# Attention and feed-forward in one kernel: batch one's V in two wide loads spread by TensorE, half-height mask matmuls, column sums in 32-column strips

## The chip, the core and the metric

The kernel runs on one core of one Trainium2 chip. The core has five engines with queues of their own: TensorE (PE: matmuls, and weight loads as PEld), VectorE (DVE), ScalarE (ACT), GpSimd (POOL) and SyncE (SP), which here issues all loads, stores and DMA transposes of the usual path. Sixteen DMA engines move the data. Each engine works through its own list in order; semaphores hold an instruction back until what it reads is there. The metric is device time in microseconds (us), lower is better. The kernel before takes 307.41 us (median of 3 runs, 306.68 to 308.96).

## What is computed

Sliding-window attention over 8 batches, 8 heads, 576 tokens, head size 64, and behind it a feed-forward layer over all 4608 tokens:

```
scores = q @ k.T / 8                      # per batch and head, 576 x 576
scores = where(|i - j| <= 32, scores, -1e9)
attn   = softmax(scores);  x = attn @ v   # heads side by side: 4608 x 512
h      = relu(x @ w_in)                   # w_in  512 x 2048
out    = (s * h * h + b) @ w_out          # w_out 2048 x 512;  s, b are single numbers
```

Since b is one number, its part of the output is b times the column sums of w_out, the same for every token.

## The kernel before, in words

**Planner.** The program is a list of tasks, each for one engine (`add`), with the tiles it reads and writes, an estimated cost and a key. `plan()` sets the tasks in order by list scheduling: it takes again and again the task that can start first by its estimates, and among equals the one with the lower key. `emit()` writes every engine's tasks in that order with the waits that are needed. So a change of one task's cost, key or tiles can move tasks everywhere behind it.

**Batch one (index 0 in the code).** Its q and k are loaded head pair by head pair (`load_pair`, four tokens to a partition, pieces of 1 KB), cast to bfloat16, transposed by TensorE through PSUM (`turn_pair`) and copied to QT and KT. `pair_scores` opens both halves of a PSUM bank with a matmul of the identity by SHUT (L920), which holds 0 inside the window and a huge negative number outside, and adds the scores of 64 x 64 blocks (L914) on top; ScalarE takes the exponential (L959). The last 64 tokens come by a tile of their own ("t", L656) and `late_scores`. V of a batch is handled in units of 128 tokens: `load_v` (L589) loads a unit with one token to a partition, pieces of 64 floats, 256 bytes; `cast_v` (L597, L598) casts it into VB, whose 65th column per head is 1, so that attention-times-V (L839, `av_part`) also gives the softmax's sums. EV0 names the engines of the casts. A unit's result is divided by its sums on VectorE (L861, L863), transposed back by TensorE (L870) and copied to XT (L878), the input of the feed-forward layer. `first_units` puts these steps in order for batch one.

**Order of the loads.** ORDER0 lists what follows q and k of batch one on SyncE: V units v0 to v4, the tail tile t and halves of the first two quarters of w_in (w0a, w0b, w1a, w1b). ORDER1 goes on with batch two (index 1), the other quarters of w_in, and w_out (o0a to o3b). Weights are loaded as float32 into a ring of staging tiles and cast by GpSimd (L564).

**Warm-up matmuls.** `stir` places matmuls without use (L614) at places named in STIR.

**Feed-forward.** `s1` computes 128 rows of x @ w_in per step (L1097), ScalarE the relu (L1104), VectorE the square (L1110). `second` computes the product with w_out for 512 tokens by seven half-size products (L1154) instead of eight; its weights need differences of blocks of w_out (`weight_sums`, L1126). `constant` computes the column sums: 16 matmuls of a matrix of ones by the 16 row blocks of w_out (L1228), two to a task, all added up in one PSUM bank; VectorE multiplies by b into CVEC (L1231), which the output step adds (L1170). FIRST orders the first layer of the first 512 tokens by quarters of w_in.

**Later batches.** From the fourth batch on (PAIRS, LONG) q and k are transposed by DMA (L749), the loads are held back until certain attention steps are done (`paced`), and the last results reach XT by DMA transposes too (L887). The five last batches are treated as one long sequence.

Of the kernel before, what the change touches and what calls it, by code (L numbers as in the profile page):

```python
# [5 lines left out]
F32 = mybir.dt.float32  # L6
# [6 lines left out]
D = 64  # L13
H = 8
# [13 lines left out]
ORDER0 = ("v0", "w0a", "v1", "t", "w0b", "v2", "v3", "w1a", "v4", "w1b")  # L28
# [20 lines left out]
EV0 = ("dve", "act", "pool", "dve", "pool")  # L49
# [6 lines left out]
        ("turn", 3, "q"): 1, ("turn", 3, "k"): 1, ("scores", 2): 1, ("scores", 3): 1, ("av", 0): 1}  # L56
# [266 lines left out]
def bass_sliding_window_symmetric__then__act_starrelu_kernel(  # L323
# [23 lines left out]
    with ExitStack() as es:  # L347
# [49 lines left out]
        IDENT = sb((128, 128), BF16, "ident")  # L397
        GT = [sb((128, 16, 512), BF16, "gt") for _ in range(2)]
# [4 lines left out]
        CVEC = sb((128, DM), F32, "cvec")  # L403
        SB128 = sb((128, 2), F32, "sb128")
# [95 lines left out]

        for i in range(4):
            add("dve", lambda e, i=i: e.tensor_scalar(SHUT[:, i, :], MASK[:, :], -OUTSIDE, OUTSIDE, ALU.mult, ALU.add), 150,
                reads=[("MASK", 0, 0), ("MASK", 0, 64)], writes=[("SHUT", i)], key=-95.0)
# [75 lines left out]
        def load_v(c, u, key, eng, waits=()):  # L579

            vs = number(c, u) % NUNIT
            ts = tiles(c, u)
            at = [tile_at(c, t) for t in ts]
            if len(at) == 2 and at[0][0] == at[1][0]:
                at = [at[0] + (0, 128)]
            else:
                at = [x + (64 * i, 64) for i, x in enumerate(at)]
            n = sum(x[3] for x in at)
            add(eng, [lambda e, b=b, j=j, p0=p0, m=m: e.dma_start(  # L589
                VST[p0:p0 + m, vs, :, :], v[b, :, 64 * j:64 * j + m, :].rearrange("h p d -> p h d"))  # L590
                for b, j, p0, m in at],
                (650.0 if eng == "sp" else 500.0) * len(at), writes=[("VST", vs)], key=key, dma=("l", n // 2, 21.5), waits=waits)
            land["v", c, u] = g.tasks[-1]
# [7 lines left out]

        def load_pair(name, pr, load_key):
# [7 lines left out]
        def stir(spot, res, view, key):  # L610

            n = STIR.get(spot, 0)
            if n:
                add("pe", [lambda e: e.matmul(view, lhsT=ONESW[:, :], rhs=ONESW[:, :].rearrange("p (one c) -> p one c", one=1)  # L614
                                              .to_broadcast((128, 4, 128)), start=True, stop=True) for _ in range(n)],
                    n * (427.0 if spot == ("turn", 0, "q") else 240.0), reads=["ONESW"], writes=[res], key=key - 0.05)
# [19 lines left out]
        def part(b, which, load_key, key, banks, slack):  # L636
# [17 lines left out]
            if which == "t":  # L654
# [3 lines left out]
                    for src, p0 in ((q, 0), (k, 64))], 1000.0, writes=stgr, key=load_key, dma=("l", 64, 21.5))  # L658
# [246 lines left out]
        def pair_scores(b, pr):  # L905
# [3 lines left out]
            if b == 0:  # L909
# [10 lines left out]
            add("pe", [lambda e, hp=hp: e.matmul(bank[:, hp, :], lhsT=IDENT[:, :], rhs=SHUT.rearrange("p u c -> p (u c)"),  # L920
                                                 start=True, stop=False, skip_group_check=True) for hp in (0, 1)],
                440.0, reads=["IDENT"] + [("SHUT", i) for i in range(4)], writes=[(name, 0), (name, 1)], key=key - 0.01)
# [72 lines left out]
        def attention():  # L995
# [228 lines left out]
        def constant():  # L1224

            for i in range(8):
                f0 = 2 * i
                add("pe", [lambda e, fc=fc: e.matmul(SC[:, 0, :], lhsT=ONESW[:, :], rhs=WOUT_BF[:, fc, :],  # L1228
                                                     start=(fc == 0), stop=(fc == 15)) for fc in (f0, f0 + 1)],
                    440, reads=["ONESW", ("Wout", i // 2, i % 2)], writes=[("SC", 0)], accum=i > 0, key=P2[0, 0] - 4.0 + 0.1 * i)  # L1230
            add("dve", lambda e: e.tensor_scalar(CVEC[:, :], SC[:, 0, :], SB128[:, 1:2], None, ALU.mult),  # L1231
                680, reads=[("SC", 0), ("SB128", 1)], writes=[("CVEC", x) for x in (0, 1)], key=P2[0, 0] - 2.0)

# [273 lines left out]
```

## Time and profile before

| | |
|---|---|
| median of 3 runs | 307.41 us |
| profiled execution: time / span in the profile | 308.89 us / 307.2 us |
| TensorE busy (PE) | 294.9 us, 96% |
| weight loads (PEld) | 213.4 us, 69% |
| VectorE / ScalarE / GpSimd busy | 233.2 / 156.7 / 66.4 us |
| moved by DMA | 54.30 MB |
| column sums L1228 | 16 matmuls, 49.5 to 57.6 us |
| mask matmuls L920 | 16 matmuls, 8 pairs |

The span runs from the first to the last instruction of one execution. A line of the timeline gives start, duration, engine, source line, operation, output and input tiles, the shape, and in brackets the idle time ahead of it with what ended it. A matmul's duration contains its way through the array, so that successive matmuls overlap: what one costs in a stream is the distance of the starts. `sc`, `o`, `avn`, `w` are PSUM tiles of two banks each. In the table of stages the numbers are the stretch in us, its length, the busy time of each engine (and its instructions), the granted TensorE clock as a share of full speed, the mean busy share of the DMA engines (over 1 where packets overlap), and GB/s.

### The profile page before, as it was taken

What the parts mean: (1) busy time and instruction counts of PE and PEld (TensorE: products, weight loads), DVE (VectorE), ACT (ScalarE), POOL (GpSimd) and SP (SyncE); (2) the same over time, 40 slices, a digit from 0 to 9 for tenths busy, and PEclk for the clock granted to TensorE, in tenths of its full rate; (3) what the DMA queues carried; (4) which work ended last, traced back from release to release, by engine and by line L of the source; (5) the groups of instructions that cost most, each with busy time, mean ns of one, the idle gap of its engine ahead of it and who ended that gap; (6) DMA issues with size and microseconds to landing.
All of it is one profiled execution on the core that took longest, in us unless ns stands there. A gap on an engine that the chain in (4) does not pass through costs nothing.

```text
span 307.2 us, 8786 instructions
## 1 busy us (share of the span) xinstructions
PE 294.9 (96%) x3837; PEld 213.4 (69%) x3837; DVE 233.2 (76%) x401; ACT 156.7 (51%) x244; POOL 66.4 (22%) x79
## 2 busy tenths in 40 slices
PE   8879899999999999999999999989999999999994
PEld 3458687798888887666766666656666666666783
DVE  3556788699879697989798768995877776566673
ACT  3746775685895564655554544542554433333200
POOL 5344587300000270055047000450000000000000
PEclk9979999999999999999999999999999999999999
DMA  7999999999994997999699679999513110210223
GB/s 204 290 246 302 325 291 370 268 227 273 159 232 125 239 202 160 279 201 178 184 255 198 132 172 273 186 201 150 153 21 88 53 47 31 74 34 2 69 70 107
DMA packets 120152, 54.30 MB, mean 177 GB/s; under 512 B 94816, under 2 KB 115936, under 8 KB 120112
## 3 DMA queue, kind: packets, MB, share of 16 engines
q1 hardware_dynamic: 120112, 53.72, 75.0%
q8 instruction: 31, 0.51, 0.8%
q14 instruction: 9, 0.07, 0.1%
HBM read 36.70 MB, written 9.44 MB: 150 GB/s over the span
## 4 chain that ended last, share of the span: by engine, by line
PE 79%; SPq 4%; DMA 3%; DVE 2%; issue 1%; POOL 0%
PE w L1097 36%; PE o L1154 31%; PE avn L839 4%; SPq L714 3%; DMA stg<-in_moe_w_in_dram 2%; PE sc L1154 2%; PE sc L781 2%; PE avn L870 1%; PE sc L1228 1%; DMA vst<-in_v_dram 1%; DVE outs L1170 1%; DVE gt L1110 1%; SPq L887 0%; SPq L707 0%; POOL win L564 0%
## 5 line engine op out<-in xcount | busy, mean ns | idle before, releaser
L1097 PE MATMUL w<-xt,win 128*128 128x512 bf16 (+4 forms) x832 | 145.7, 316 | 1.3 <-POOL win L564 1.3
L1104 ACT ACTIVATE r<-w 128x512 bf16<-128x512 f32 (+2 forms) x148 | 86.6, 586 | 105.6 <-PE w L1097 103.9
L1097 PEld LDWEIGHTS w<-xt,win 128*128 128x128 bf16 x832 | 75.6, 99 | 35.9 <-POOL win L564 1.9
L1110 DVE TENSOR_TENSOR gt<-r 128x1024 bf16<-128x1024 bf16 (+3 forms) x100 | 63.6, 639 | 24.9 <-ACT r L1104 24.2
L1154 PE MATMUL o<-wout,gt 128*128 128x256 bf16 x528 | 66.5, 273 | 0.0
L1154 PEld LDWEIGHTS o<-wout,gt 128*128 128x128 bf16 x528 | 50.8, 98 | 13.3
L733 POOL CAST nat<-stg 128x1024 bf16<-128x1024 f32 (+2 forms) x28 | 33.7, 1202 | 78.8 <-DMA stg<-in_q_dram 65.0
L809 ACT ACTIVATE ex<-sc 128x1024 bf16<-128x1024 f32 (+1 forms) x29 | 29.7, 1023 | 12.4 <-PE avn L839 10.8
L1154 PE MATMUL o<-tw,gt 128*128 128x256 bf16 x272 | 34.6, 273 | 0.0
L1154 PEld LDWEIGHTS o<-tw,gt 128*128 128x128 bf16 x272 | 26.2, 98 | 7.0
L1170 DVE SCALAR_TENSOR_TENSOR outs<-o,sb,cvec 128x512 f32<-128x512 f32 (+1 forms) x36 | 25.7, 715 | 4.3 <-PE o L1154 4.3
L1170 DVE SCALAR_TENSOR_TENSOR outs<-o,sb,outs 128x512 f32<-128x512 f32 (+1 forms) x27 | 19.3, 716 | 6.7 <-PE o L1154 6.6
L1146 DVE TENSOR_TENSOR gt<-gt 128x1024 bf16<-128x1024 bf16 (+1 forms) x26 | 23.8, 916 | 0.4
L813 DVE TENSOR_TENSOR ex<-ex,mask 128x1024 bf16<-128x1024 bf16 (+1 forms) x29 | 22.5, 775 | 0.6
L863 DVE TENSOR_TENSOR xn<-avn,rec 128x512 bf16<-128x512 f32 (+1 forms) x31 | 21.3, 687 | 0.7
L839 PE MATMUL avn<-vb,ex 64*64 64x65 bf16 x944 | 19.9, 197 | 1.9 <-issue 1.6
L839 PEld LDWEIGHTS avn<-vb,ex 64*64 64x64 bf16 x944 | 13.0, 106 | 11.5 <-issue 8.0
L598 DVE CAST vb<-vst 128x512 bf16<-128x512 f32 (+1 forms) x30 | 13.1, 444 | 9.5 <-DMA vst<-in_v_dram 9.5
L1154 PE MATMUL o<-tw,gsum 128*128 128x256 bf16 x136 | 17.7, 273 | 0.0
L1154 PEld LDWEIGHTS o<-tw,gsum 128*128 128x128 bf16 x136 | 12.8, 98 | 3.3
L1146 DVE TENSOR_TENSOR gsum<-gt 128x1024 bf16<-128x1024 bf16 x18 | 13.2, 731 | 0.3
L878 ACT COPY xt<-avn 128x512 bf16<-128x512 bf16 (+2 forms) x19 | 10.0, 533 | 4.8 <-PE avn L870 4.8
(119 smaller groups left out, 225.4 us busy)
## 6 DMA issues: line engine op xcount, KB each, us to landing
vst<-in_v_dram SPq DMA_DIRECT2D x32, 256.0 KB, 4.8
out_dram<-outs SPq DMA_DIRECT2D x32, 256.0 KB, 3.6
stg<-in_k_dram SPq DMA_DIRECT2D x24, 256.0 KB, 6.5
stg<-in_q_dram SPq DMA_DIRECT2D x5, 1024.0 KB, 6.0
stg<-in_moe_w_in_dram SPq DMA_DIRECT2D x8, 512.0 KB, 7.4
stg<-in_moe_w_out_dram SPq DMA_DIRECT2D x8, 512.0 KB, 7.4
stg<-in_q_dram SPq DMA_DIRECT2D x4, 512.0 KB, 8.2
stg<-in_k_dram SPq DMA_DIRECT2D x4, 512.0 KB, 8.4
```

The costliest lines, as they stand in the source:

```text
L598: (lambda e: e.tensor_copy(VB[0:n, vb, :, 0:D], VST[0:n, vs, :, :])),
L733: (lambda e, dst=dst, src=src: e.tensor_copy(dst, src)),
L809: add("act", lambda e, dst=flat_dst, src=flat_src: e.activation(dst, src, AF.Exp, bias=0.0, scale=0.125), 190 + 0.833 * 512 * len(hs), rea ...
L813: add("dve", lambda e, flat=flat, mask=mask: e.tensor_tensor(flat, flat, mask, ALU.mult), 130 + 0.53 * 512 * len(hs), reads=[("E", ei, hp, ...
L839: return [lambda e: e.matmul(av[64 * x:64 * x + 64, h, 0:D + 1], lhsT=buf[64 * g:64 * g + 64, h % 2, h // 2, c:c + 64], rhs=VB[64 * g:64 * ...
L863: add("dve", lambda e: e.tensor_tensor(XN[xi][0:p1, :].rearrange("p (a c) -> p a c", a=H), av[0:p1, :, 0:D], REC[ri][0:p1, :].rearrange("p ...
L1097: add("pe", [lambda e, g=g, kc=kc: e.matmul(wt[:, g, :], lhsT=WIN_BF[:, kc, (f0 + g) * 128:(f0 + g + 1) * 128], rhs=XT[:, kc, t0 % XR:t0 % ...
L1104: add("act", lambda e: e.activation(rt, wt, AF.Relu, bias=0.0, scale=1.0), 190 + 0.833 * ng * nt, reads=[("W", wb)], writes=[("R1", rb, ha ...
L1110: add("dve", lambda e: e.tensor_tensor(GT[gs][:, f1:f1 + nf, g0:g0 + nt], rr, rr, ALU.mult), 130 + 0.55 * nf * nt, reads=[("R1", rb, x) fo ...
L1146: add("dve", lambda e: e.tensor_tensor(dst, x, y, op), 1240.0 if half is None else 690.0, reads=reads, writes=writes, key=k)
L1154: add("pe", [lambda e, g=g, j=j, dst=dst: e.matmul(dst, lhsT=lhs[:, g, 128 * j:128 * j + 128], rhs=rhs[:, g, :], start=first and g == 0 an ...
L1170: add("dve", lambda e, src=src, dst=dst, other=other: e.scalar_tensor_tensor(dst, src, SB128[:, 0:1], other, ALU.mult, ALU.add), 200 + 1.0 ...
```

## The change

**V of batch one.** Units 0 to 3 (512 tokens) come by two loads "va" and "vb" of 256 tokens, each on all 128 partitions with two neighbouring tokens to a partition, so that a piece is 512 bytes. VectorE casts such a load into a NAT tile (VCAST). Four matmuls with a 0/1 matrix SPREAD, 64 rows each, bring the tokens to one per partition in two PSUM banks (AVN 0 and 1, for both loads), and ScalarE (units 0 and 2) or VectorE (units 1 and 3) copies each unit from PSUM to VB. Unit 4 (64 tokens) is loaded and cast as before. "va" and "vb" stand at the head of ORDER0. The warm-up ahead of the first attention-times-V grows from 1 to 5 matmuls and waits for the first spread.

**Masks.** The opening matmul of `pair_scores` takes 64 rows instead of 128 for each half: TWICE holds two 64 x 64 identities side by side, and the two halves of SHUT are equal, so either half of the rows gives the whole mask.

**Column sums.** Four groups of four matmuls: a group's matmuls write 32-column strips of the array, each its own 32 partitions of one PSUM bank, with ones of 32 columns. ScalarE copies the strips to CVEC, one float32 matmul with a matrix of 1/32 (PART) adds the four strips for all partitions, and VectorE multiplies by b as before.

Two cost entries of the planner are changed as well (27.0 for loads on 64 partitions).

```diff
-ORDER0 = ("v0", "w0a", "v1", "t", "w0b", "v2", "v3", "w1a", "v4", "w1b")
+ORDER0 = ("va", "vb", "w0a", "t", "w0b", "w1a", "v4", "w1b")
-EV0 = ("dve", "act", "pool", "dve", "pool")
+VCAST = ("dve", "dve")
+EV0 = ("act", "dve", "act", "dve", "pool")
-        ... ("scores", 3): 1, ("av", 0): 1}
+        ... ("scores", 3): 1, ("av", 0): 5}
+        for p0 in (0, 64):
+            add("dve", lambda e, p0=p0: e.tensor_copy(
+                TWICE[p0:p0 + 64, :].rearrange("p (a c) -> p a c", a=2),
+                IDENT[p0:p0 + 64, p0:p0 + 64].rearrange("p (a c) -> p a c", a=1).to_broadcast((64, 2, 64))), 120,
+                reads=["IDENT"], writes=[("TWICE", p0)], key=-95.5)
+        def load_runs(y, key):
+            add("sp", lambda e: e.dma_start(
+                VST[:, 2 * y:2 * y + 2, :, :].rearrange("p u h d -> p (u h d)").rearrange("p (h c) -> p h c", h=H),
+                v[0, :, 256 * y:256 * y + 256, :].rearrange("h (p i) d -> p h (i d)", i=2)),
+                600.0, writes=[("VST", 2 * y), ("VST", 2 * y + 1)], key=key, dma=("l", 64, 27.0))
+        def spread_runs(y, key, homes):
+            ni = take("nat", NNAT)
+            rows, eng = NAT[ni], VCAST[y]
...
+            add("pe", [lambda e, i=i, u=u: e.matmul(
+                homes[u][1], lhsT=SPREAD[64 * u:64 * u + 64, 128 * i:128 * i + 128],
+                rhs=rows[64 * u:64 * u + 64, 512 * i:512 * i + 512], start=(i == 0), stop=(i == 1))
+                for i in (0, 1) for u in (0, 1)], 480.0, reads=[("NAT", ni), ("SPREAD", 0), ("SPREAD", 1)],
+                writes=[x[0] for x in homes], key=key)
+            land["spread", y] = g.tasks[-1]
+            for u in (0, 1):
+                vb, eng = number(0, 2 * y + u) % NVB, EV0[2 * y + u]
+                dst, src = VB[:, vb, :, 0:D], homes[u][1].rearrange("p (h d) -> p h d", h=H)
+                add(eng, ..., {"act": 617.0, "dve": 680.0}[eng],
+                    reads=[homes[u][0]], writes=[("V", vb)], key=key + 0.1 * u)
-            add("pe", [lambda e, hp=hp: e.matmul(bank[:, hp, :], lhsT=IDENT[:, :], rhs=SHUT.rearrange("p u c -> p (u c)"),
+            add("pe", [lambda e, hp=hp: e.matmul(bank[:, hp, :], lhsT=TWICE[64 * hp:64 * hp + 64, :],
+                                                 rhs=SHUT[64 * hp:64 * hp + 64, :, :].rearrange("p u c -> p (u c)"),
-                stir(("av", u), res[0], bank[:, 0, :], -25.0 + u)
+                stir(("av", u), res[0], bank[:, 0, :], -25.0 + u, [land["spread", 0]])
+                elif t in ("va", "vb"):
+                    y = "ab".index(t[1])
+                    load_runs(y, nxt())
+                    spread_runs(y, -28.0 + 3 * y, banks1)
-            for i in range(8):
-                f0 = 2 * i
-                add("pe", [lambda e, fc=fc: e.matmul(SC[:, 0, :], lhsT=ONESW[:, :], rhs=WOUT_BF[:, fc, :],
-                                                     start=(fc == 0), stop=(fc == 15)) for fc in (f0, f0 + 1)],
+            for r in range(4):
+                add("pe", [lambda e, r=r, c=c: e.matmul(SC[32 * c:32 * c + 32, 0, :], lhsT=ONESW[:, 0:32], rhs=WOUT_BF[:, 4 * r + c, :],
+                                                        start=(r == 0), stop=(r == 3), skip_group_check=True) for c in range(4)],
+            add("act", lambda e: e.copy(CVEC[:, :], SC[:, 0, :]), 617.0, ...)
+            add("pe", lambda e: e.matmul(SC[:, 1, :], lhsT=PART[:, :], rhs=CVEC[:, :], start=True, stop=True), 1000.0, ...)
-            add("dve", lambda e: e.tensor_scalar(CVEC[:, :], SC[:, 0, :], SB128[:, 1:2], None, ALU.mult),
+            add("dve", lambda e: e.tensor_scalar(CVEC[:, :], SC[:, 1, :], SB128[:, 1:2], None, ALU.mult),
```

More of the change, by code (lines that the diff above doesn't have):

```diff
@@ L55 @@
 STIR = {("turn", 0, "q"): 7, ("scores", 0): 3, ("turn", 1, "q"): 2, ("turn", 1, "k"): 1, ("turn", 2, "q"): 1, ("turn", 2, "k"): 1,
[L56 removed]
+        ("turn", 3, "q"): 1, ("turn", 3, "k"): 1, ("scores", 2): 1, ("scores", 3): 1, ("av", 0): 5}
 OUTSIDE = -1.0e38
@@ L403, in bass_sliding_window_symmetric__then__act_starrelu_kernel @@
         CVEC = sb((128, DM), F32, "cvec")
+        PART = sb((128, 128), F32, "part")
         SB128 = sb((128, 2), F32, "sb128")
@@ L499, in bass_sliding_window_symmetric__then__act_starrelu_kernel @@
             band(MASK[p0:p0 + 64, :], ONESW[p0:p0 + 64, :], ("MASK", 0, p0), 0, 64, -96)
+        for p0 in (0, 64):
[3 more added lines that the diff above has]
+                reads=["IDENT"], writes=[("TWICE", p0)], key=-95.5)
+        add("dve", lambda e: e.memset(SPREAD[:, :], 0.0), 150, writes=[("SPREAD", u) for u in (0, 1)], key=-59)
+        for u in (0, 1):
+            add("dve", lambda e, u=u: e.tensor_copy(
+                SPREAD[64 * u:64 * u + 64, :].rearrange("p (i x) -> p i x", i=2)[:, :, 0:128:2],
+                IDENT[64 * u:64 * u + 64, 64 * u:64 * u + 64].rearrange("p (i c) -> p i c", i=1).to_broadcast((64, 2, 64))), 150,
+                reads=["IDENT"], writes=[("SPREAD", u)], key=-59)
         for i in range(4):
@@ L591, in load_v @@
                 for b, j, p0, m in at],
-                (650.0 if eng == "sp" else 500.0) * len(at), writes=[("VST", vs)], key=key, dma=("l", n // 2, 21.5), waits=waits)
+                (650.0 if eng == "sp" else 500.0) * len(at), writes=[("VST", vs)], key=key, dma=("l", n // 2, 21.5 if n > 64 else 27.0), waits=waits)
             land["v", c, u] = g.tasks[-1]
@@ L608, in load_pair, with stir @@
                 600.0, writes=stgr, key=load_key, dma=("l", 16, 60.0))
-        def stir(spot, res, view, key):
+        def stir(spot, res, view, key, waits=()):
             n = STIR.get(spot, 0)
@@ L615, in stir @@
                                               .to_broadcast((128, 4, 128)), start=True, stop=True) for _ in range(n)],
-                    n * (427.0 if spot == ("turn", 0, "q") else 240.0), reads=["ONESW"], writes=[res], key=key - 0.05)
+                    n * (427.0 if spot == ("turn", 0, "q") else 240.0), reads=["ONESW"], writes=[res], key=key - 0.05, waits=waits)
         def turn_pair(name, pr, key, banks, eng, slack):
```

23 lines of the change are left out of this document (19 added, 4 removed).

## The prediction

> **What bounds the kernel now.** I read the page first, then its busy times by stage.
>
> ```profile
> span 307.2 us, 8786 instructions
> ...
> PE   8879899999999999999999999989999999999994
> ...
> DMA  7999999999994997999699679999513110210223
> ```
>
> ```profile
> core 0: us, PE busy (x) PEld busy (x) DVE busy (x) ACT busy (x) POOL busy (x), PEclk, DMA share, GB/s
> 0.00:20.30 20.30, 15.96 (x240) 8.37 (x241) 8.56 (x27) 11.54 (x18) 8.72 (x24) 0.98 0.96 249
> 20.30:36.63 16.33, 14.58 (x246) 12.16 (x238) 12.09 (x22) 10.52 (x19) 7.64 (x8) 0.92 1.07 302
> 36.63:57.98 21.35, 20.96 (x360) 16.36 (x361) 16.87 (x32) 12.99 (x25) 15.73 (x17) 1.00 1.11 309
> 57.98:300.00 242.02, 240.33 (x2975) 174.03 (x2974) 193.72 (x318) 121.68 (x184) 34.29 (x30) 1.00 0.70 152
> ```
>
> From 58 us to 300 us TensorE is busy for 240.33 of 242.02 us; nothing of the change lies there. What can be won is ahead of 58 us, where the 16 DMA engines are full (share about 1 in each row) and TensorE is not. The order of time on TensorE, and the casts on GpSimd that let it go on, say which transfer counts:
>
> ```profile
> 14.26 0.70 PE L839 MATMUL sc<-vb,ex 64*64 64x65 bf16 x24
> 15.42 0.72 PE L839 MATMUL o<-vb,ex 64*64 64x65 bf16 x32 [0.46 <-ACT vb L597]
> ...
> 20.30 2.90 PE L1097 MATMUL w<-xt,win 128*128 128x224 bf16 x16
> ...
> 26.47 0.94 PE L1097 MATMUL w<-xt,win 128*128 128x224 bf16 x8 [0.21 <-POOL win L564]
> ...
> 36.63 0.94 PE L1097 MATMUL w<-xt,win 128*128 128x224 bf16 x8 [1.05 <-POOL win L564]
> ...
> 57.38 0.60 PE L1228 MATMUL sc<-wout,onesw 128*128 128x512 bf16 x2
> ```
>
> ```profile
> 16.87 1.04 POOL L564 CAST win<-stg 128x1024 bf16<-128x1024 f32 x1 [0.99 <-DMA stg<-in_moe_w_in_dram]
> ...
> 25.37 1.04 POOL L564 CAST win<-stg 128x1024 bf16<-128x1024 f32 x1 [1.87 <-DMA stg<-in_moe_w_in_dram]
> ...
> 35.54 1.04 POOL L564 CAST win<-stg 128x1024 bf16<-128x1024 f32 x1 [0.39 <-DMA stg<-in_moe_w_in_dram]
> ...
> 56.28 1.04 POOL L564 CAST wout<-stg 128x1024 bf16<-128x1024 f32 x1 [0.77 <-DMA stg<-in_moe_w_out_dram]
> ```
>
> At 26.47 and 36.63 TensorE starts when a w_in cast ends, and each cast starts when its DMA lands. At 57.38 the last two column sums start 0.06 us after the last w_out cast ends (56.28 + 1.04 = 57.32). So the load queue sets the pace at three marks, the last at 57.3 us.
>
> **Part 1, V of batch one.** Four loads of 256 KB in 256-byte packets become two of 512 KB in 512-byte packets. Windows of 2 us and 1 us with one packet size show both neighbours (1024-byte pieces of q and k, then V), a third the second pair of V loads, and the whole start:
>
> ```profile
> DMA packets 735, 0.71 MB, mean 355 GB/s; under 512 B 42, under 2 KB 735, under 8 KB 735
> ```
> ```profile
> DMA packets 948, 0.24 MB, mean 238 GB/s; under 512 B 948, under 2 KB 948, under 8 KB 948
> ```
> ```profile
> DMA packets 578, 0.17 MB, mean 167 GB/s; under 512 B 565, under 2 KB 565, under 8 KB 578
> ```
> ```profile
> DMA packets 14150, 9.79 MB, mean 272 GB/s; under 512 B 8325, under 2 KB 12421, under 8 KB 14147
> ## 3 DMA queue, kind: packets, MB, share of 16 engines
> q1 hardware_dynamic: 14147, 9.75, 99.8%
> ```
>
> 256 KB at 238 and 167 GB/s are 1.1 and 1.6 us; I take 1.3, so the four cost 5.2 us (4.4 to 6.3). No row has 512-byte packets. Bounds per 512 KB: 1.5 us at the 355 GB/s of 1024-byte packets, 2.2 us at 238. On a line through packet spacings of 16.9 ns (1 us over 948, times 16) and 43.5 ns (2 us over 735, times 16) a 512-byte packet takes 25.8 ns, and 1024 of them on 16 engines 1.65 us. I take 3.3 us for two (3.0 to 4.4). **The queue gets 1.9 us shorter** (0 to 3.3), and since it is 99.8% busy to 36 us, all behind it lands 1.9 us sooner. The Trainium skill (DMA: Bandwidth & Descriptors, Specifications) puts the least size for line rate at 512 B; by that the two would cost 3.0 us and the gain be 2.2 us, and no row of this run tests it.
>
> What comes earlier in the queue moves the other way: both V loads now stand before the first w_in half, so the tail tiles and the second half land 3.3 - 2.6 = 0.7 us later. That cast (16.87, ending 17.9) then ends at 18.6, still ahead of 20.30, so this costs nothing. SyncE issues two loads fewer, and GpSimd loses the cast of unit 2.
>
> The compute on V gets longer. New are, per load, one cast of 128x1024 on VectorE, four matmuls (64 rows by 512 columns, two side by side) and two evictions from PSUM. Both loads use the same two AVN banks, so the second spread waits until both evictions of the first are done. In the built program ScalarE's eviction of unit 0 stands behind all exponentials of batch one:
>
> ```profile
> 13.78 1.08 ACT L959 ACTIVATE ex<-o 128x256 bf16<-128x256 f32 x2
> 14.73 0.63 ACT L597 CAST vb<-vst 128x512 bf16<-128x512 f32 x1
> ```
> ```profile
> 3.24 0.59 DVE L502 TENSOR_SCALAR shut<-mask 128x128 bf16<-128x128 bf16 x4 [1.28 <-POOL mask L492]
> ...
> 15.25 0.69 DVE L863 TENSOR_TENSOR xn<-sc,rec 128x512 bf16<-128x512 f32 x1
> ...
> 29.70 0.68 DVE L646 CAST nat<-stg 128x1024 bf16<-128x1024 f32 x1
> ```
>
> The exponentials end at 14.86; the eviction takes about 0.6 us (nearest row: the 0.63 cast), to 15.4. The second spread ends at 15.9, and TensorE's in-order queue holds the first attention-times-V (14.26) behind it: 1.6 us late. The second (15.42) follows at 16.3, 0.9 us late. VectorE first evicts unit 3 (0.69 by the row at 15.25), so unit 1 is normalised about 1.4 us late. But unit 2 no longer waits for its own V, whose cast ended at 19.4, and the first w_in matmuls start about where they did (20.1 against 20.30). The four extra warm-up matmuls (0.9 us) lie in TensorE's wait for the second spread. The new 0/1 tiles on VectorE fit into its 1.28 us idle before 3.24. The start itself I cost at 0; if that cover fails it is up to 1.6 us, and the first mark still hides most of it, because the cast of 25.37 now ends at 24.5.
>
> A half clock hits TensorE here, after a stretch in which it was busy for 1.52 of 3.41 us:
>
> ```profile
> 15.98:19.39 3.41, 1.52 (x44) 0.97 (x34) 0.90 (x2) 2.79 (x6) 1.66 (x2) 1.00 1.03 235
> 19.39:22.80 3.41, 3.30 (x46) 2.65 (x47) 2.76 (x5) 0.67 (x2) 1.04 (x1) 0.50 0.89 242
> ```
>
> The later attention work fills that stretch, so it may stay at full clock. That is worth up to 1.7 us on TensorE, but at 36.63 TensorE waits for its weight cast anyway: I count 0.
>
> **Part 2, masks.** Two 128-row matmuls become two of 64 rows that can run side by side. Rows for the price, and for a change of array shape:
>
> ```profile
> 41.91 1.28 PE L1097 MATMUL w<-xt,win 128*128 128x160 bf16 x16
> 43.03 0.39 PE L870 MATMUL o<-ident,xn 128*128 128x128 bf16 x4
> ...
> 47.62 1.28 PE L1097 MATMUL w<-xt,win 128*128 128x160 bf16 x16
> 48.83 0.70 PE L839 MATMUL avn<-vb,ex 64*64 64x65 bf16 x24
> 49.47 1.04 PE L1228 MATMUL sc<-wout,onesw 128*128 128x512 bf16 x4
> 50.34 0.39 PE L870 MATMUL o<-ident,xn 128*128 128x128 bf16 x4
> ```
>
> Four 512-column matmuls take 0.87 us (49.47 to 50.34), 0.22 each. The same 16 matmuls take 1.12 us before a 128x128 follower and 1.21 before a 64x64 one: a change of shape costs 0.09 us. Of the eight pairs seven lie ahead of the 36.63 mark and count nothing; the eighth saves 0.2 us.
>
> **Part 3, column sums.** Before: 16 matmuls at 0.22, 3.5 us. After: four groups of four in 32-column strips. A group costs 0.22 (all side by side) to 0.87 us (none); no row has 32-column strips, I take 0.25. Seven more changes of shape are 0.6 us. One float32 matmul over 512 columns follows, 0.2 us if as fast as bfloat16; with no row for it I take 0.9 (four times) as upper bound and value. Together 2.5 us: TensorE saves 1.0 us. The Trainium skill (TensorE: Matmul & The Clock Gate, Part 3) gives a speedup of 2.38 for three 32-column strips of 512 columns; by that, as an estimate, three such matmuls take 0.65 / 2.38 = 0.27 us, a group of four about 0.3, and the sum would be 2.7 us instead of 2.5; no row of this run shows it. ScalarE's copy of 0.6 us lies under 16 first-layer matmuls that stand between.
>
> **The sum.** At 36.63 the gain is 1.9. From there to the last group TensorE's work shrinks by 0.2 (mask) and by 1.8 (14 old sums, 3.0 us, against three groups, 0.75, and five changes, 0.45), and grows by 0.9, since eight more first-layer matmuls now stand ahead of that group. It arrives 1.9 + 1.1 = 3.0 us sooner, at 54.4; the last w_out cast ends at 57.3 - 1.9 = 55.4. **A new wait of 1.0 us takes the place of what parts 2 and 3 saved.** Behind it: the last group costs 0.25 + 0.2 against 0.5 before, the float32 matmul adds 0.9, and 0.9 of first-layer work is already done. Net 1.9 to 2.0 us. The profiled execution took 308.89 us; less 2.0 it would be 306.9. It lies 1.5 us above the median of 307.41; I give the median: **305.4 us**.
>
> **Rivals.** *The wait does not form* (w_out lands another microsecond sooner, or 512-byte packets run at 355 GB/s and better): the gain is 3.0 to 3.5 us, 304.1. For it: the first V pair ran at 238 GB/s, the second at 167. Against it: 57.38 sits on the cast today. *512-byte packets are no quicker per byte* (V at 238 GB/s before and after): the queue gains 0 to 0.5, TensorE is let go at the same marks, 307.0. *Column strips run one after another*: 4 x 0.87 + 0.6 + 0.9 = 5.0 us against 3.5; the wait at the last group swallows part, gain 0.5, 306.9. *Slower, by key transposes that come too late*: one batch already waits there.
>
> ```profile
> 208.09 0.32 PE L839 MATMUL avn<-vb,ex 64*64 64x65 bf16 x16 [1.62 <-issue]
> ```
>
> TensorE idles 1.62 us before a score step that reads keys transposed by DMA; SyncE issues these transposes in order with stores and V loads. The planner lays all later steps out anew, and in the built program attention units stand at other places among the layers. If two more of the five batches of the long sequence stop there, 3.2 us are lost against 2.0 won: 308.6; it decides from the second extra stop on, and three give 310.3. For it: SyncE's order there differs by a V load and a store. Against it: the loads are released by attention steps that move with TensorE.
>
> **How the numbers follow.** Chances: forecast 0.48, no wait 0.22, slow packets or serial strips 0.17, transposes 0.13. One per cent is 3.1 us, about what a measurement of this kernel tells from no change; its three runs spread by 2.3 us. The forecast itself spans 304.5 to 306.4; with the rivals the range is 303.2 to 308.5. Faster by over 1% (below 304.3): most of the no-wait case and an edge of the forecast, 0.24; slower by over 1%: three late stops, 0.08; else 0.68.
>
> **What would show it.** The two V loads finish within 3.5 us of each other's queue time; the w_in cast of 35.54 starts near 33.6; TensorE waits about 1 us for GpSimd's w_out cast before the last strip group near 55 us; a group of four lasts 0.25 us; first attention-times-V at about 15.9. Wrong it is if that cast does not move, if strips take 0.87 us a group, or if idle time beyond 58 us differs from today's 1.7 us.

## The result and the profile after

| | |
|---|---|
| kernel before, beside it | 308.72 us median (20 runs, 306.68 to 310.9) |
| changed kernel | 307.11 us median (20 runs, 305.86 to 308.48) |
| ratio | 0.9954, 95% interval 0.9932 to 0.9977: 1.4 us less (0.7 to 2.1) |
| profiled execution: time / span | 308.19 us / 306.3 us (before 308.89 / 307.2) |

The time lies inside the range of the prediction, 1.7 us above its 305.4. Of these, 1.3 us are the base: three runs had put the kernel before at 307.41, twenty put it at 308.72. The rest is the gain, by these medians 1.6 instead of 2.0 us. The gain came nearly right by steps that were wrong, as the experiments show. Ratios and fits leave out the few runs that took over 1.5% more than the fastest of their kernel; none of these forty did.

The page of the changed kernel, its span and the 40 slices of TensorE and DMA:

```profile
span 306.3 us, 8830 instructions
...
PE   8989999899999999999999999998999999999994
...
DMA  7999999999992997999799779997803111200223
```

The picture is that of before: TensorE nearly full behind the start, the DMA engines close to full for the first 90 us.

Its busy times by stage, in the columns of the table in the prediction, cut where TensorE starts weight matmuls as it did at the first marks of that table:

```profile
0.00:20.95 20.95, 17.89 (x252) 8.37 (x253) 11.24 (x35) 11.21 (x18) 8.18 (x23) 0.97 0.97 259
20.95:36.59 15.64, 15.19 (x281) 12.44 (x273) 11.42 (x23) 11.63 (x22) 8.57 (x9) 0.93 1.13 306
36.59:57.98 21.39, 19.53 (x343) 15.57 (x338) 17.84 (x32) 13.58 (x26) 15.38 (x17) 1.00 1.11 303
57.98:300.00 242.02, 240.79 (x2974) 174.17 (x2972) 195.09 (x318) 120.88 (x183) 34.43 (x30) 1.00 0.70 153
```

TensorE reaches its first weight matmuls at 20.95 us (20.30 before), so there is no gain at the first mark. At the second the times are equal, 36.59 and 36.63, but the order is not: by 36.59 TensorE has done two score steps and a mask pair that stood behind the mark before, 1.0 us of work. The order of time on TensorE, and GpSimd's casts:

```profile
14.01 0.60 PE L634 MATMUL avn<-nat,spread 64*128 64x512 bf16 x4 [0.19 <-DVE nat L632]
...
16.55 0.64 PE L884 MATMUL sc<-vb,ex 64*64 64x65 bf16 x18
...
18.56 0.40 PE L705 MATMUL w<-ident,nat 128*128 128x128 bf16 x4 [0.76 <-POOL nat L691]
...
20.95 2.79 PE L1147 MATMUL w<-xt,win 128*128 128x224 bf16 x16
...
25.07 0.39 PE L965 MATMUL sc<-shut,twice 64*128 64x512 bf16 x2
25.39 1.07 PE L1147 MATMUL w<-xt,win 128*128 128x128 bf16 x16
...
36.59 1.71 PE L1147 MATMUL w<-xt,win 128*128 128x224 bf16 x16
...
47.87 0.40 PE L1279 MATMUL sc<-wout,onesw 128*32 128x512 bf16 x4
48.20 0.70 PE L884 MATMUL avn<-vb,ex 64*64 64x65 bf16 x24
...
57.17 0.40 PE L1279 MATMUL sc<-wout,onesw 128*32 128x512 bf16 x4 [0.95 <-POOL wout L580]
...
59.26 1.02 PE L1283 MATMUL sc<-cvec,part 128*128 128x512 f32 x2
60.12 0.39 PE L705 MATMUL avn<-ident,nat 128*128 128x128 bf16 x4
...
61.22 1.04 PE L1204 MATMUL o<-wout,gt 128*128 128x256 bf16 x8
```

```profile
19.25 1.04 POOL L580 CAST win<-stg 128x1024 bf16<-128x1024 f32 x1 [0.75 <-DMA stg<-in_moe_w_in_dram]
...
35.09 1.04 POOL L580 CAST win<-stg 128x1024 bf16<-128x1024 f32 x1 [0.22 <-DMA stg<-in_moe_w_in_dram]
...
56.08 1.04 POOL L580 CAST wout<-stg 128x1024 bf16<-128x1024 f32 x1 [1.01 <-DMA stg<-in_moe_w_out_dram]
```

The predicted wait ahead of the last strip group is there, 0.95 us at 57.17. But in this execution it is there because the queue gained only 0.2 us (the last w_out cast starts at 56.08 instead of 56.28). A second execution of each kernel, below, shows other marks. The price of the sums is as forecast or better: a group takes 0.33 us with its changes of shape (47.87 to 48.20), the float32 matmul 0.86 us (59.26 to 60.12). Four groups and the matmul are 2.2 us against 3.5 before, so TensorE saves 1.3 us. A mask pair takes 0.32 us (25.07 to 25.39).

The last line of TensorE's timeline above, the first matmul of the second layer at 61.22 us, is the best mark for comparing executions: TensorE's matmuls ahead of it are the same in number and shape, but for those of the change. Before, it stood here:

```profile
61.56 1.92 PE L1154 MATMUL o<-wout,gt 128*128 128x256 bf16 x16
```

By this mark the changed kernel is only 0.3 us ahead. Another 0.5 us of the 0.9 us between the two spans is idle time behind 58 us (1.23 us after, 1.69 before).

### The profile page after: what moved, and what is told of

It reads as the page before. It is cut to its first block, busy times and chain, and to the rows that moved or that the text cites. A ratio compares the mean times of both kernels' runs of the same rounds, so it can differ in the third digit from the quotient of the medians.

```text
span 306.3 us, 8830 instructions
## 1 busy us (share of the span) xinstructions
PE 295.7 (97%) x3851; PEld 212.3 (69%) x3851; DVE 237.2 (77%) x409; ACT 157.3 (51%) x246; POOL 66.6 (22%) x78
## 4 chain that ended last, share of the span: by engine, by line
PE 73%; DMA 17%; SPq 3%; POOL 3%; DVE 1%; ACT 1%; issue 0%; POOLq 0%
PE o L1204 31%; PE w L1147 30%; DMA stg<-in_moe_w_out_dram 5%; DMA stg<-in_k_dram 4%; PE avn L884 3%; DMA stg<-in_q_dram 3%; DMA stg<-in_moe_w_in_dram 3%; PE sc L1204 2%; POOL nat L778 2%; SPq L759 2%; PE sc L826 2%; DMA kt<-nat 2%; PE avn L915 1%; POOL wout L580 1%; PE avn L718 1%; ACT ex L1005 1%
## 5 line engine op out<-in xcount | busy, mean ns | idle before, releaser
L1160 DVE TENSOR_TENSOR gt<-r 128x1024 bf16<-128x1024 bf16 (+3 forms) x100 | 62.1, 628 | 23.8 <-ACT r L1154 23.1
L614 DVE CAST vb<-vst 128x512 bf16<-128x512 f32 (+1 forms) x28 | 13.8, 498 | 1.6 <-DMA vst<-in_v_dram 1.6
```

The lines of the kernel that those rows point to most:

```text
L614: (lambda e: e.tensor_copy(VB[0:n, vb, :, 0:D], VST[0:n, vs, :, :])),
L1160: add("dve", lambda e: e.tensor_tensor(GT[gs][:, f1:f1 + nf, g0:g0 + nt], rr, rr, ALU.mult), 130 + 0.55 * nf * nt, reads=[("R1", rb, x) fo ...
```

## The experiments

**Theories.** The prediction's: the load queue sets the pace up to 58 us, so part 1 brings 1.9 us and parts 2 and 3 only make TensorE wait. First rival: TensorE is as late by its own work and other waits, so its saved work counts and the queue's doesn't. Second rival: the parts matter little, and each edit draws another order from the planner, with other stalls far behind. All ratios are to the kernel before, run in the same job; 0.001 is 0.3 us.

**Each part alone.** Part 1 alone takes back the masks and sums, part 2 alone the V loads and sums, part 3 alone the V loads and masks.

```diff
 # part 1 alone                         # in ORDER0, EV0, load_runs, spread_runs as changed
-        matmul(bank[:, hp, :], lhsT=TWICE[64 * hp:64 * hp + 64, :], rhs=SHUT[64 * hp:64 * hp + 64, ...])
+        matmul(bank[:, hp, :], lhsT=IDENT[:, :], rhs=SHUT...)
-        for r in range(4): add("pe", four matmuls into 32-column strips) ; copy ; float32 matmul
+        for i in range(8): add("pe", two matmuls over 128 columns)
 # parts 2 and 3 alone: also
-ORDER0 = ("va", "vb", "w0a", "t", "w0b", "w1a", "v4", "w1b")
+ORDER0 = ("v0", "w0a", "v1", "t", "w0b", "v2", "v3", "w1a", "v4", "w1b")
```

> Kernel before with the V part alone (wide loads, spread, 5 warm-up matmuls); masks and column sums as before. Theory A (the w_out casts set the pace at 57 us, and what the V loads save is given back before them, as in the profile of after, where the last w_out cast starts 0.2 us sooner): last w_out cast at 55.9 to 56.4 us, gain 0 to 0.5 us. Theory B (the saving of 1.9 us normally reaches w_out, and the profile of after was an unlucky execution): last w_out cast at 54.2 to 54.8 us, gain 1.5 to 2 us, since no work on TensorE is added behind 20 us.

Measured: ratio 1.0013 (0.9983 to 1.0044).

> Kernel before with the 64-row mask matmuls alone. Theory A: same time within 0.3 us, since seven of the eight pairs lie ahead of a wait for a load and the eighth saves 0.2 us. Rival (a change of array shape costs more than the 0.09 us taken): a pair costs 0.4 us or more from its start to the next start, and the time rises by 0.3 to 1 us.

Measured: ratio 1.0039 (1.0003 to 1.0074).

> Kernel before with the column sums in strips alone. Theory A: a group of four takes about 0.33 us, the saved TensorE time turns into a wait for the last w_out cast of 0.5 to 1.2 us ahead of the last group, and the time falls by 0 to 0.4 us. Rival (the wait does not bind; what TensorE saves comes out at the end): gain of 1.0 us or more.

Measured: ratio 0.9983 (0.9944 to 1.0021).

So no part alone is clearly faster, and part 2 alone is slower. In the profile of part 1 alone the last w_out cast starts at 54.99 us, 1.3 earlier than before. The last sums wait 0.44 us for it and start at 56.09, and the second layer starts at 60.28, 1.3 us earlier too: in this execution the shorter queue, or the full clock that TensorE had all the way from 20 to 37 us, does reach TensorE. But it is the second shortest of its twelve (308.44 us), and their median is not below that of the kernel before (309.69 and 308.89). So neither theory's forecast came true.

**The changed kernel and the kernel before, once more,** for the spread of the marks between executions of one program.

```diff
 # no line differs: the changed kernel (e4), the kernel before (f4)
```

> The changed kernel once more, for a second profile and a time beside its three parts. Theory A: last w_out cast at 55.7 to 56.4 us, wait ahead of the last strip group 0.7 to 1.2 us, time 1 to 2 us below before; the parts alone do not add up to it. Theory B: last w_out cast near 54.5 us.

Measured: ratio 0.9946 (0.9915 to 0.9977), profiled 307.23 us.

> Kernel before once more, for a second profile: how far the marks move from one execution to the next. Expected: last w_out cast within 0.7 us of 56.3, stall ahead of the attention step near 206 us anywhere from 0.2 to 1.9 us.

Measured: one execution, 309.27 us, span 307.5. The stall near 206 us is absent.

The last w_out cast and TensorE's column sums in this second execution of the kernel before:

```profile
56.27 1.04 POOL L564 CAST wout<-stg 128x1024 bf16<-128x1024 f32 x1 [0.72 <-DMA stg<-in_moe_w_out_dram]
```
```profile
49.30 1.21 PE L1097 MATMUL w<-xt,win 128*128 128x160 bf16 x15 [1.10 <-issue]
...
58.87 0.59 PE L1228 MATMUL sc<-wout,onesw 128*128 128x512 bf16 x2
...
63.02 1.15 PE L1154 MATMUL o<-wout,gt 128*128 128x256 bf16 x9
```

The cast ends at 57.31 as in the first one. But TensorE comes to the last sums at 58.87, 1.6 us after it: here its own lateness is the bound, not the queue. Of the 1.5 us that it is later than in the first execution, 1.1 are one gap, at 49.30, for which the profile names no cause; so this one execution does not show that TensorE is always so late. The changed kernel's second execution, in the same two views:

```profile
54.33 1.25 POOL L580 CAST wout<-stg 128x1024 bf16<-128x1024 f32 x1 [0.53 <-DMA stg<-in_moe_w_out_dram]
```
```profile
57.28 0.40 PE L1279 MATMUL sc<-wout,onesw 128*32 128x512 bf16 x4
...
61.33 1.04 PE L1204 MATMUL o<-wout,gt 128*128 128x256 bf16 x8
```

Now the queue has its forecast gain (54.33, 1.95 earlier than before) and there is no wait for the cast. Yet the last group starts at 57.28 and the second layer at 61.33, no sooner than in the execution where it waited (57.17 and 61.22). TensorE had lost the time in front. Its waits from 16 to 60 us, in this execution (engine, what it waited for, us in total, times, longest):

```profile
PE w L705 <- POOL nat L691: 1.6, 1, 1.6
PE sc L959 <- DVE kt L697: 1.1, 1, 1.1
PE sc L915 <- DVE xn L908: 0.7, 1, 0.7
```

Those are the tail tile, which the V loads have pushed back (before, TensorE waited for it 0 and 0.65 us in the two executions), a copy of keys, and a normalised unit. None is a weight cast.

**Two parts at a time.**

```diff
 # g1, h2: masks taken back              # g2: column sums taken back       # g3: V loads taken back
-lhsT=TWICE[64*hp:64*hp+64, :] ...      -four strip groups + float32       -ORDER0 = ("va", "vb", ...)
+lhsT=IDENT[:, :] ...                   +sixteen full matmuls              +ORDER0 = ("v0", "w0a", "v1", ...)
```

> The changed kernel with the masks taken back to the 128-row identity (parts 1 and 3 without part 2). Theory A (the parts have prices of their own; the masks are worth 0.2 us at most): as the changed kernel, ratio 0.995 to 0.996 of the kernel before, and the last w_out cast between 54 and 56 us. Theory B (what decides is how the planner lays out the steps behind 58 us, and each edit draws a new layout): the ratio has nothing to do with the parts; between 0.995 and 1.004, and where it is over 1.000 the excess shows as stalls of 0.3 to 2 us at single steps behind 140 us. Theory C (adding up the single parts: V +0.4 us, sums -0.5 us): 1.000.

Measured: ratio 0.9928 (0.9902 to 0.9953).

> Parts 1 and 3 without part 2, once more. Theories P and Q: 0.991 to 0.994, as the first time. Theory R: 0.9945 to 0.995.

Measured, the same kernel again in another job: 0.9965 (0.9924 to 1.0006).

> The changed kernel with the column sums taken back to 16 full matmuls (parts 1 and 2 without part 3). Theory A (with w_out landing 1 to 2 us sooner TensorE is late by its own work, so the 1.0 us of the column sums is paid in full): ratio 0.998, that is 1 us slower than the changed kernel. Theory B (layout): anything between 0.995 and 1.006. Theory C (adding up the single parts: V +0.4, masks +1.2 us): 1.005.

Measured: 1.0018 (0.9982 to 1.0054).

> The changed kernel with V of batch one loaded as before, in four loads of 256 KB (parts 2 and 3 without part 1). Theory A (the load queue sets the pace up to the last w_out cast; without the shorter queue the column sums only wait for that cast): ratio 1.000, last w_out cast at 56.2 to 56.8 us. Theory B (layout): anything between 0.995 and 1.006 with the same cast time. Theory C (adding up: masks +1.2, sums -0.5 us): 1.002.

Measured: 1.0003 (0.9973 to 1.0034).

All eight combinations have now been run. A least-squares fit to the 218 single times of these kernels and of the kernel before beside them, with a level for each job and terms for every pair and for all three, gives each part's effect as a mean over the four combinations of the other two (interval by resampling):

| part | mean effect, us | 95% interval |
|---|---|---|
| 1, V loads | -0.7 | -1.1 to -0.2 |
| 2, masks | +0.4 | 0.0 to +0.9 |
| 3, column sums | -1.5 | -1.9 to -1.1 |

The 1.3 us of TensorE work that the sums save lie inside their interval. The parts don't simply add up. Parts 1 and 3 together are 1.3 us better than their sum (0.4 to 2.2): the V loads bring nothing without the sums (0.0, -0.6 to +0.6) and 1.3 us with them (0.7 to 2.0), the sums 0.9 us without the V loads (0.2 to 1.5) and 2.2 with them (1.6 to 2.7). Parts 1 and 2 are 1.0 us better than their sum (0.1 to 1.8): part 2 costs 0.9 us without part 1 (0.3 to 1.6) and nothing beside it.

**The queue emptied.** The strongest test of what bounds the stretch ahead of 58 us: the 1.2 MB of batch two's V are not loaded at all, in the changed kernel (g4) and in the kernel before (h3).

```diff
                 elif step[0] == "v":
-                    load_v(1, int(step[1]), nxt(), "sp")
```

> The changed kernel without the five loads of batch two's V (1.2 MB; batch two's attention then reads what lies in the buffer, so its part of the output is left out). They stand among the w_in and w_out halves, at about 300 GB/s worth 3.9 us of queue. Theory A (the load queue sets when TensorE gets past the column sums): the last w_out cast starts near 51 us, the last strip group comes 2 to 3 us sooner, the time falls by 2 us or more against the changed kernel (ratio below 0.990). Theory D (with w_out 1 to 2 us sooner TensorE is already late by its own work and by waits for casts and normalisations): the last strip group moves by under 1 us, and the ratio stays within 0.992 to 0.997.

Measured: 0.9935 (0.9911 to 0.9958), last w_out cast at 50.00 us.

> The kernel before without the five loads of batch two's V (1.2 MB; batch two's attention reads what lies in the buffer, so its part of the output is left out). The last w_out cast starts near 50 us instead of 56.3. Theory A of the prediction (the load queue alone sets when TensorE gets past 57 us): the time falls by 2 us or more, ratio below 0.9935. Theory D (TensorE and the queue arrive at nearly the same time there, so that neither alone is worth much; TensorE's own work and its waits for casts and normalised units ahead of 50 us bound as well): ratio 0.997 to 1.001.

Measured: 1.0026 (0.9998 to 1.0053), last w_out cast at 50.06 us.

w_out is there 6 us sooner, and neither kernel gains clearly: the changed one stands within 0.6 us of where it stood (0.9946 and 0.9954), the one before is no faster at all. In the kernel before without those loads:

```profile
50.06 1.04 POOL L564 CAST wout<-stg 128x1024 bf16<-128x1024 f32 x1 [0.77 <-DMA stg<-in_moe_w_out_dram]
```
```profile
53.96 1.91 PE L1096 MATMUL w<-xt,win 128*128 128x256 bf16 x16
...
57.25 1.91 PE L1153 MATMUL o<-wout,gt 128*128 128x256 bf16 x16
```

The second layer starts at 57.25, but the planner has put 48 first-layer matmuls behind that start and eight transposes ahead of it. At 1.74 us for sixteen such matmuls (53.96 to 55.70, where the next step starts) and 0.44 us for the transposes, TensorE has the work of the old mark done at about 62.0 us (an estimate from these rows), against 61.56 and 63.02 with the loads. So TensorE is as late there without that queue, by its own work and its other waits. TensorE's waits from 16 to 60 us, in the profiled execution of before first and then without those loads:

```profile
PE sc L839 <- POOL vb L598: 1.4, 1, 1.4
PE w L1097 <- POOL win L564: 1.3, 2, 1.0
PE o L870 <- DVE xn L863: 0.5, 1, 0.5
PE sc L920 <- ACT ex L959: 0.4, 1, 0.4
```
```profile
PE sc L839 <- POOL vb L598: 1.2, 1, 1.2
PE avn L938 <- ACT kt L651: 0.7, 1, 0.7
PE w L660 <- POOL nat L646: 0.6, 1, 0.6
PE sc L920 <- ACT ex L959: 0.6, 1, 0.6
...
PE w L1096 <- POOL win L564: 0.2, 1, 0.2
```

The 1.3 us for w_in casts shrink to 0.2, and 0.7 for keys and 0.6 for the tail tile stand in their place: 3.6 us in four lines against 3.3 in these five and 0.5 in two that are left out. The removed wait had others just behind it. The second execution of the kernel before, with all its loads, has nearly the same list (0.2 for w_in casts, 0.7 for keys, 0.6 for the tail tile), so the list itself changes from one execution to the next and doesn't price the loads. (And since the planner lays out the rest differently without those tasks, the runs exclude a gain of 2 us but don't price the queue to a tenth.)

**What part 2 costs.** The kernel before with its instructions unchanged and only the planner's cost of a mask pair lowered (f1): its order on TensorE and SyncE is that of part 2 alone. And the changed kernel with that entry set back (h1): behind 17 us its order on TensorE is that of the changed kernel.

```diff
 # f1, on the kernel before              # h1, on the changed kernel
-                440.0, reads=["IDENT"]  -                240.0, reads=[("TWICE", 0)
+                240.0, reads=["IDENT"]  +                440.0, reads=[("TWICE", 0)
```

> Kernel before, with nothing but the planner's cost entry of the mask matmuls set from 440 to 240; every instruction is that of before, TensorE's and SyncE's order is that of the masks-only kernel. Theory C (what the new order does to the stalls behind 60 us moves the time as much as the edits themselves): time 0.5 to 1.5 us above before, with stalls over 0.5 us ahead of a matmul near 142 us or 207 us, as in the masks-only run (0.98 and 1.88 us). Rival (the order is neutral, and the masks-only run was slow by its 64-row matmuls): same as before within 0.4 us.

Measured: 1.0025 (0.9991 to 1.006).

> The changed kernel, all three parts, with only the planner's cost entry of a mask pair set back from 240 to 440. TensorE's order behind 17 us is that of the changed kernel; ahead of it a few steps of the start change places, to the order of the kernel with parts 1 and 3 alone (0.9928). Theory P (the 0.7 us that part 2 costs comes from the order that the entry draws): 0.991 to 0.993. Theory Q (it comes from the half-height instructions, which leave TensorE idle longer ahead of 16 us): 0.995. Theory R (part 2 costs nothing and 0.9928 was a lucky draw): 0.9945 to 0.995.

Measured: 0.9963 (0.993 to 0.9997).

The waits of TensorE from 60 to 302 us in part 2 alone, then with the entry alone:

```profile
PE avn L845 <- DMA kt<-nat: 1.8, 1, 1.8
PE avn L876 <- DVE xn L869: 0.8, 1, 0.8
```
```profile
PE avn L870 <- DVE xn L863: 0.8, 1, 0.8
```

The wait of 0.8 us for a normalised unit comes with the order, whether the masks take 64 rows or 128; the kernel before had none there. Part 3 alone has a wait of the same kind and length and is no slower for it. That part 2 alone costs by the order is therefore likely and not shown: the entry alone gives +0.8 us, an interval that just includes zero. In the changed kernel the entry moves steps of the start only, and there it makes no difference (0.9963, the changed kernel 0.9946 and 0.9954). The 0.9928 of parts 1 and 3 looks like a lucky draw: its repeat gave 0.9965, and the two intervals overlap.

**Two tries at a better version.** In f2 the tail tile stands ahead of the first w_in half, because TensorE had waited 0.8 to 1.6 us for it. In f3 the planner is told that w_out lands later, so that eight more matmuls stand ahead of the last strip group.

```diff
 # f2
-ORDER0 = ("va", "vb", "w0a", "t", "w0b", "w1a", "v4", "w1b")
+ORDER0 = ("va", "vb", "t", "w0a", "w0b", "w1a", "v4", "w1b")
 # f3
-                dma=("l", 16, 87.0))
+                dma=("l", 16, 87.0 if which == "in" else 100.0))
```

> Changed kernel with the tail tile's two loads ahead of the first w_in half. Theory D (in the changed kernel the start was not free: TensorE waits 0.8 to 1.6 us for the cast of the tail tile at 17 to 18.6 us, and the first w_in matmul starts 0.7 to 1.1 us later than before): that wait falls under 0.3 us, the first w_in matmul starts at 20.0 to 20.7 us, bound by the second w_in half, and the time falls by 0.3 to 0.8 us against the changed kernel. Rival (later waits swallow it): same as the changed kernel within 0.3 us.

Measured: 0.9982 (0.9953 to 1.0012).

> Changed kernel with the planner told that w_out lands later (100 instead of 87 per unit); the last strip group then has eight more first-layer matmuls (0.87 us) ahead of it. If the wait ahead of that group (0.95 us in the first profile of the changed kernel, none in the second) sets the end: wait under 0.2 us and 0.3 to 0.9 us off the changed kernel. If it doesn't, since TensorE is as late by itself: same within 0.3 us.

Measured: 0.9948 (0.9916 to 0.9981).

In the first the wait for the tail tile is gone, and another has taken its place on TensorE's timeline:

```profile
21.62 0.61 PE L915 MATMUL sc<-ident,xn 128*128 128x128 bf16 x4 [1.05 <-DVE xn L908]
22.02 1.70 PE L1147 MATMUL w<-xt,win 128*128 128x224 bf16 x8
```

TensorE waits 1.05 us for a normalised unit, and the first weight matmuls start at 22.02 us instead of 20.95. The second equals the changed kernel. No version tried beats it beyond doubt.

## Why the prediction was right or wrong

- **Price of a V load.** Forecast 1.65 us, bounds 1.5 to 2.2. A window of 1 us inside the V loads of the changed kernel's second execution holds almost nothing but 512-byte packets:

```profile
DMA packets 575, 0.29 MB, mean 293 GB/s; under 512 B 6, under 2 KB 574, under 8 KB 575
```

  512 KB at 293 GB/s are 1.8 us, so two take 3.6 instead of 3.3. The queue gains 5.2 - 3.6 = 1.6 us, not 1.9. The 5.2 us for the four old loads is too much as well. Its 167 GB/s are the end of the second pair, where the engines run dry: the queue's share is 94% there, and in the second half of that window 73%. A microsecond earlier, from 16.2 to 17.2 us, the same loads ran at 246 GB/s at a share of 127%. At 238 and 246 GB/s the four cost 4.3 to 4.4 us, and the queue gains 0.7 to 0.8 us. The Trainium skill (DMA: Bandwidth & Descriptors, Specifications) puts line rate at 512 B and up. Here 512-byte packets ran at 293 GB/s and the 1024-byte ones of the prediction at 355, so the measurement decides: 512 B is not yet the full rate.
- **"All behind it lands 1.9 us sooner."** The term was mis-sized. The last w_out cast started at 56.28 and 56.27 before, at 56.08 and 54.33 after, a gain of 0.2 to 1.95 us. Over the nine profiles of kernels with part 1 and with all loads it starts at 55.5 in the mean (54.33 to 56.53), over the six without part 1 at 56.3 (55.7 to 56.7). That is 0.7 us, what the queue gains by the prices above.
- **"So this costs nothing"** (the second w_in half): wrong. The cast was to move from 16.87 to 17.6 and started at 19.25, 2.4 us later. In the second executions it is 19.62 against 18.44, so 1.8 us in the mean. The tail tile shares the delay, and TensorE waits 0.76 us for it at 18.56 (1.6 in the second execution). The first weight matmuls start at 20.95 and 21.36 against 20.30 and 21.16, 0.4 us later in the mean, where the forecast had 0.2 earlier. The first attention-times-V at 16.55 (forecast 15.9) is part of the same term.
- **"So the load queue sets the pace at three marks"**: this is the step that failed. It was read from one execution in which TensorE and the last cast met within 0.06 us. In another execution of the same program TensorE came 1.6 us after the cast, and with 1.2 MB taken out of the queue w_out was there 6 us sooner and the time no less. Beside the old sums the V loads brought 0.0 us, where the step had 1.9 for them with or without the sums. Queue, tail tile, key copies and normalised units all end within a microsecond or so of each other.
- **"A new wait of 1.0 us takes the place of what parts 2 and 3 saved"**: the wait was seen in one of two executions (0.95 us), for the other reason that the queue had not gained. On the mean the sums' saving is not swallowed: it is the larger part of the gain, -1.5 us (-1.9 to -1.1), where their rows save 1.3.
- **"It lies 1.5 us above the median of 307.41; I give the median"**: this step took off 1.5 us on the strength of three runs. Twenty put the median at 308.72, close to the profiled 308.89, so 1.3 of the 1.7 us by which 305.4 is off come from here. The 306.9 ahead of that step lies 0.2 us from the measured 307.11; with the gain's steps as they were, that is luck.
- **Prices on TensorE** were nearly right: a strip group 0.33 us with both changes of shape (forecast 0.25 and 0.09 each, 0.43), the float32 matmul 0.86 (0.9), the mask pair 0.12 us cheaper (0.2). The Trainium skill's 2.38 (TensorE: Matmul & The Clock Gate, Part 3) had led to 0.3 us a group; with the two changes that would be 0.48, so 0.33 is nearer to the 0.25; no row parts the group from its changes.
- **Masks cost nothing:** right in the changed kernel. That the edit of a cost entry alone can move the time was named for the transposes, not for this part; alone it cost 1.2 us.
- **Rivals.** The strips ran side by side, so "serial strips" is out, and so is "slow packets" (293 GB/s against 238 and 246). "The wait does not form" happened in the second execution without its gain of 3 us, because TensorE was late. The key transposes are an open lottery: the stall at 208 us was 1.62 us before, 1.2 in the changed kernel, 0.1 in its second execution and absent from the second one of before. Beyond 58 us idle time is 242.02 - 240.79 = 1.23 us after and 1.69 before, so 0.5 us of this one profile's difference lies there. The low end of the range, 303.2, has no working; the lowest rival is 304.1.
- **The half clock** was counted as 0, and the text thought it might go. In this execution it did not, although the stretch ahead is fuller than before (2.31 of 3.40 us busy against 1.52 of 3.41):

```profile
16.40:19.80 3.40, 2.31 (x81) 1.53 (x82) 2.35 (x5) 1.40 (x4) 2.15 (x3) 1.00 1.10 288
19.80:23.20 3.40, 3.32 (x61) 2.65 (x59) 2.08 (x4) 2.52 (x5) 2.18 (x3) 0.50 1.19 219
```

  Over all runs it did get shorter. It lasts 3.4 and 6.8 us in the two executions of the kernel before, 3.4 in both of the changed kernel, and is absent from that of part 1 alone. The mean granted clock is 0.995 in 121 runs of kernels with part 1 and 0.989 in 176 without; half clock for 3.4 us takes off 3.4 x 0.5 / 306 = 0.0055, so part 1 goes with about one such stretch less. Among runs of one kernel, 0.0055 more clock goes with 0.6 us less time (0.4 to 0.7). So a part of what the V loads bring may come by the clock and not by the queue. No run separates the two, and part 1 alone has the higher clock without being faster.

What stays open: how much of part 1 is queue and how much is clock; why the 1.2 us that part 2 costs alone are gone beside part 1; that the entry then moves steps of the start only fits, but no run separates the moved steps.

## What to carry to other kernels

A wait that ends last in one profiled execution is a bound only if the next ones are far behind: take a second profile of the same program before building a sum on it, and look at how late the engine would be without the wait. Where queue and engine are that close, a shorter queue is worth next to nothing until the engine's work shrinks too, and the saved work brought less without the shorter queue (0.9 against 2.2 us): here the two together brought 1.3 us more than their sum. With a planner, run the cost entry alone, because a change of order can be larger than the edit.

## What the runs showed of the hardware that was not expected

VectorE's products and GpSimd's casts lengthened each other. The same three VectorE products (two of 128x320, one of 128x512) and two GpSimd casts lay nearly apart in the first execution of the changed kernel and side by side in the second. First execution, VectorE, then GpSimd:

```profile
32.89 1.08 DVE L1160 TENSOR_TENSOR gt<-r 128x320 bf16<-128x320 bf16 x3
```
```profile
33.66 1.21 POOL L580 CAST win<-stg 128x1024 bf16<-128x1024 f32 x1 [2.38 <-DMA stg<-in_moe_w_in_dram]
35.09 1.04 POOL L580 CAST win<-stg 128x1024 bf16<-128x1024 f32 x1 [0.22 <-DMA stg<-in_moe_w_in_dram]
```

Second execution, VectorE and the key copy behind it, then GpSimd:

```profile
33.05 2.56 DVE L1160 TENSOR_TENSOR gt<-r 128x320 bf16<-128x320 bf16 x3
35.53 1.21 DVE L697 COPY kt<-avn 128x1024 bf16<-128x1024 bf16 x1
```
```profile
32.60 2.73 POOL L580 CAST win<-stg 128x1024 bf16<-128x1024 f32 x2 [1.74 <-DMA stg<-in_moe_w_in_dram]
```

The three products take 2.56 us instead of 1.08, the two casts 2.73 instead of 2.25. The key copy behind them, itself no longer than in the first execution beside a cast (1.21 and 1.22 us), is what TensorE waited 1.1 us for. So a weight that lands 1.5 us earlier (its cast at 32.60, in the kernel before at 34.11) can delay TensorE by the engine that it meets. The Trainium skill (SBUF — State Buffer, SBUF: two separate sides) says that the two engines share a pair of ports by an exclusive lock for a whole instruction. The lengthening agrees with that in sign; one such meeting doesn't test the rule.
